# Set attention with inducing points and a hardswish layer: earlier second load, constants on another engine, the verdict's steps moved in a written-out order

## The chip, the cores and the metric

The kernel runs on one core of one Trainium2 chip. The metric is the device time of one execution in microseconds (us); lower is better. The times are the median of several executions; beside them stands one execution that the hardware profiler recorded, with its own time and its span, which runs from the first to the last instruction.

## What is computed

```python
B, N, m, C = 4, 12480, 32, 128            # x: (B, N, C), inducing: (m, C), w_in: (128, 2048), w_out: (2048, 128)

def mab(q, kv):
    s = (1 / sqrt(C)) * (q @ kv.transpose(0, 2, 1))
    a = exp(s - s.max(-1, keepdims=True))
    a /= a.sum(-1, keepdims=True) + 1e-09
    return a @ kv

h = mab(I, x)                             # I: the inducing points, once per batch
y = mab(x, h).reshape(B * N, C)           # 49920 rows of 128
u = y @ w_in
out = (u * clip(u + 3.0, 0.0, 6.0) / 6.0) @ w_out     # float32, (49920, 128)
```

## The kernel before

**Two paths.** The kernel holds a fast path, which is one straight run of instructions, and behind it a slow path, `direct_path` (from L884). The fast path does not form the hidden layer. It expands the output of the second attention and the hardswish layer in the attention weights of the 32 inducing points: a linear part, and a quadratic part that is a sum over pairs of inducing points. That holds only while some conditions are met (bounded values, sums of weights that come out as they should). The fast path counts how often they are met, and one number, the tile `bad_i`, says whether all were. At the end every engine loads `bad_i` into a register (L877) and compares it with zero (L880). If it is 0 the program ends; if it is 1, `direct_path` computes the whole result once more, straight from the definition, and writes all of `out` again.

**The order.** Tile's own scheduling is off. The string `ORDER` (L23 to L162) lists some 1590 tokens; the loop at L873 takes them one after the other and calls the function `op_<code>` with the token's numbers. That text is the program's order: each engine gets its instructions in the order of the tokens, and the waits between the engines are put in by it, so that whoever reads a buffer waits for the token that wrote it last *before it in the text*, and whoever writes a buffer waits for earlier readers. Letters at a token's end name the engine (V is VectorE, A is ScalarE, P is GpSimd). The last number or numbers of many tokens name a bank of the PSUM tile `ps` (128 partitions, 8 banks of 512 float32).

**The work.** Each of the 4 batches is cut into 6 full groups of 2048 rows and a last small one of 192 (96 partitions by 2). Per group: `X` loads x (GpSimd's queue, L408), `K` casts it to bfloat16, `T` and `Y` transpose it over TensorE, `S`, `E`, `A` and `H` are scores, exponentials and weighted sums of the first attention. Per batch, the `c` tokens make the coefficients. `cW` (L622 to L627) adds two terms into the tile `CqT` and then halves one block of it, because a pair 16 places apart is listed twice. Per group again: `Z` to `Ra` are the second attention, `W` spreads a tile by DMA (SyncE's queue, L680), `B` forms sums over pairs of inducing points in PSUM (L731, four banks at a time: `B.3.5.1.4.6` writes banks 4, 5, 6 and 7), `F` and `U` turn them into products, `l` and `q` multiply these with the coefficients (L776, L797), `v` copies the result out of PSUM (L811) and `O` writes it (SyncE's queue, L824). The result of a small group goes through one buffer, `osl`.

**The start.** `X.0.0.8.16` and `X.0.0.0.8` load the two halves of the first group. Between them in the order stands `i6`, which makes constants on GpSimd (L357 to L363). `i1` makes the identity matrix on GpSimd, `i7` and `i9` further constants there (L367 to L382). TensorE meanwhile runs `w` tokens, wide matmuls whose results are not used (L353, 28 of them ahead of the first transposes).

**The verdict.** `y1` to `y3` count conditions on VectorE into columns of `cnt`. The one on the sums takes two tokens: `yb` (L834) is a matmul that adds the row sums `s_all` of all 28 groups over blocks of 32 partitions, into columns 0 to 27 of a PSUM bank. `y0` (L839 to L841) subtracts from that bank what is due, `s_due` (16384 for a full group, 3072 for a small one), squares the difference, and counts where it is at most 4. `y4` (L865) adds the counts over the partitions, `y5` (L868, L870) compares the total with the number that all conditions together give, and writes `bad_i`. The order before ends in `yb.6 y0.6 y1.- y4.6 O.3.6.0.- y5.6`.

**The slow path.** For each of the 4 batches `direct_path` runs two loops on the chip, of 130 turns each (L940 and L971), over 96 rows of x a turn. Each turn is one chain, since every buffer there exists once: a first-loop turn loads 96 rows by DMA, transposes, multiplies with the inducing points, takes a maximum, two exponentials, transposes, multiplies and adds to the running sum. A second-loop turn does the same for the second attention and then the layer itself in float32:

```python
   993	                for jb in range(FB):                      # 16
   994	                    nc.tensor.matmul(up[:, jb, :TN], lhsT=w_in[:, jb * P : (jb + 1) * P], rhs=h[:, :])
   996	                nc.vector.tensor_scalar(g[:, :, :], up[:, :, :TN], 3.0, 0.0, op0=ALU.add, op1=ALU.max)
   997	                nc.vector.tensor_scalar(g[:, :, :], g[:, :, :], 6.0, 1.0 / 6.0, op0=ALU.min, op1=ALU.mult)
   998	                nc.vector.tensor_mul(g[:, :, :], g[:, :, :], up[:, :, :TN])
  1000	                for jb in range(FB):
  1001	                    nc.tensor.matmul(op[:TN, :C], lhsT=g[:, jb, :], rhs=w_out[:, jb, :], ...)
  1005	                nc.vector.tensor_copy(ot[:, :], op[:TN, :C])
  1006	                nc.sync.dma_start(out[bass.ds(r0 + row, TN), :], ot[:, :])
```

At a turn's end all engines wait for each other and for all transfers before they branch back.

Of the kernel before, what the change touches and what calls it, by code (L numbers as in the profile page):

```python
# [147 lines left out]
q.3.1.0.1.3 Zs.3.3 y2.- Rz.3.4.1 q.3.1.1.1.2 F.3.2.1.0.4 O.3.0.0.- B.3.2.0.0.4 v.3.1.0.3.V W.3.2 q.3.1.3.0.3 U.3.1.1  # L148
F.3.2.1.1.6 v.3.1.1.2.V Z.3.5.6 l.3.1.1.7.3 O.3.1.0.- q.3.1.3.1.3 F.3.2.0.1.4 F.3.2.0.0.0 q.3.2.1.0.2 q.3.1.2.0.7
q.3.1.2.1.7 Ze.3.5.6 O.3.0.1.- Zu.3.3 Zd.3.3 Ra.3.3 v.3.1.3.3.V B.3.3.0.4.0 l.3.2.0.3.2 U.3.2.0 Zs.3.4 W.3.3 q.3.2.0.0.3  # L150
v.3.1.2.7.A q.3.2.0.1.3 F.3.3.0.1.0 q.3.2.1.1.2 R.3.5.7 q.3.2.2.0.0 q.3.2.3.0.1 O.3.1.1.- U.3.2.1 Zu.3.4 v.3.2.0.3.A
F.3.3.0.0.4 Rl.3.5.7 v.3.2.1.2.V q.3.2.2.1.0 B.3.3.1.4.2 Zd.3.4 l.3.2.1.0.1 Rh.3.4.V q.3.3.0.0.7 Rz.3.5.6 q.3.3.1.0.6
U.3.3.0 v.3.2.2.0.V q.3.2.3.1.1 W.3.4 F.3.3.1.0.4 F.3.3.1.1.2 v.3.2.3.1.A l.3.3.0.7.6 B.3.4.0.2.4 U.3.3.1 Z.3.6.0
q.3.3.1.1.6 F.3.4.0.0.2 q.3.3.0.1.7 v.3.3.1.6.V Ze.3.6.0 Ra.3.4 q.3.3.2.0.1 q.3.3.2.1.1 F.3.4.0.1.4 O.3.2.1.- R.3.6.6
Zs.3.5 O.3.2.0.- q.3.4.0.0.2 q.3.3.3.0.3 q.3.3.3.1.3 Zu.3.5 Rl.3.6.6 Rz.3.6.0 v.3.3.0.7.A O.3.3.0.- B.3.4.1.6.4 U.3.4.0
l.3.3.1.1.3 Rh.3.5.V l.3.4.0.2.0 Zd.3.5 v.3.3.2.1.V F.3.4.1.1.4 W.3.5 F.3.4.1.0.6 v.3.3.3.3.V q.3.4.1.0.0 q.3.4.1.1.0
# [37 lines left out]
def kernel(  # L194
# [32 lines left out]
    with ExitStack() as es:
        es.enter_context(tc.manual_schedule())
# [393 lines left out]
        def op_cW(b, k):  # L622
            split = lambda t: t.rearrange("p (f i m) -> p f i m", f=4, m=M)
            nc.vector.tensor_add(  # L624
                CqT[:, :, :, :].rearrange("p f m i -> p f i m"), split(ps[:, k, :]), split(r6[:, :])
            )
            nc.vector.tensor_scalar_mul(CqT[:, 3, :, 3], CqT[:, 3, :, 3], 0.5)  # L627
# [239 lines left out]
        def op_y5(k):  # L867
            nc.vector.tensor_reduce(cs[:, :], ps[:1, k, :5], axis=AX.X, op=ALU.add)  # L868
# [1 line left out]
            nc.vector.tensor_scalar(bad_i[:, :], cs[:, :], good, None, op0=ALU.not_equal)  # L870
# [166 lines left out]
```

## Time and profile before

| what | value |
|---|---|
| median of 3 runs | 268.82 us (268.12 to 272.86) |
| the profiled execution, its own time | 269.06 us |
| its span, first to last instruction | 267.2 us |
| busy share of TensorE, VectorE, ScalarE, GpSimd | 94%, 87%, 88%, 29% |
| mean granted TensorE clock | 0.991 |
| last instruction that counts as work (`bad_i`, L870) | starts at 263.84 us |
| loads of `bad_i` into registers (L877) | five, one per engine, from 264.0 us, about 0.5 us each |

A line of the profile has the start in us, the length in us, the engine, the line of the program, the operation, and the tiles it writes and reads. PE is TensorE's matmuls, PEld its weight loads, DVE VectorE, ACT ScalarE, POOL GpSimd, SP SyncE; a "q" behind an engine is its queue or sequencer. In the list of groups the last numbers are the busy time in us and the mean of one in ns. `direct_path` is not in this trace: `bad_i` was 0.

### The profile page before, as it was taken

To read this page: it belongs to the slowest core of one execution; us is meant where nothing else is said; L and a number is where in the kernel's file an instruction comes from. 1 tells how busy PE (TensorE), PEld (TensorE's weight loads), DVE (VectorE), ACT (ScalarE), POOL (GpSimd) and SP (SyncE) were. 2 spreads that over 40 slices of the span, in tenths; PEclk is the share of its full clock that TensorE was granted. 3 is DMA by queue.
4 is the path that set the end of the run, shared out by engine and by line. 5 is a ranking of instruction groups with operands and counts; after the bars stand their busy time and mean duration, and the time that the engine had idled before them with its cause. 6 is when DMAs were issued, how large, how long until landed. Compare 5 with 4: busy or idle time off the path is not lost.

```text
span 267.2 us, 9566 instructions
## 1 busy us (share of the span) xinstructions
PE 251.7 (94%) x3941; PEld 198.7 (74%) x3941; DVE 233.2 (87%) x497; ACT 235.7 (88%) x390; POOL 78.5 (29%) x112
## 2 busy tenths in 40 slices
PE   8998979999998999999999999989998999999991
...
GB/s 129 397 345 401 411 379 49 306 287 199 230 383 348 275 55 308 208 237 398 346 308 238 266 387 27 244 54 235 44 241 285 205 127 241 150 248 255 323 226 184
DMA packets 26768, 66.68 MB, mean 250 GB/s; under 512 B 4032, under 2 KB 17120, under 8 KB 23520
## 3 DMA queue, kind: packets, MB, share of 16 engines
...
HBM read 27.67 MB, written 25.56 MB: 199 GB/s over the span
## 4 chain that ended last, share of the span: by engine, by line
PE 60%; DMA 11%; DVE 11%; ACT 9%; issue 5%; SPq 2%; POOL 2%; DVEq 0%; ACTq 0%; POOLq 0%
PE ps L797 26%; PE ps L776 6%; PE ps L731 5%; PE ps L445 5%; PE ps L418 4%; DMA d<-dk 4%; PE ps L596 4%; DMA xr<-in_x_dram 3%; PE ps L649 2%; DMA out_dram<-os 2%; PE ps L429 2%; PE ps L688 2%; ACT xb L412 2%; ACT xT L424 1%; DVE CqT L624 1%
## 5 line engine op out<-in xcount | busy, mean ns | idle before, releaser
L741 ACT ACTIVATE TF<-ps 128x1024 bf16<-128x1024 f32 (+1 forms) x100 | 97.4, 1018 | 2.6 <-PE ps L731 2.0
L750 DVE TENSOR_TENSOR TD<-TF,d 128x2048 bf16<-128x2048 bf16 (+1 forms) x52 | 60.4, 1172 | 3.8 <-DMA d<-dk 3.1
L797 PE MATMUL ps<-Cq,TD 128*128 128x128 bf16 (+1 forms) x784 | 56.7, 219 | 1.6 <-DVE TD L750 1.5
L797 PE MATMUL ps<-Cq,TF 128*128 128x128 bf16 (+1 forms) x784 | 56.9, 219 | 0.0
L797 PEld LDWEIGHTS <-TF 128*128 128x128 bf16 (+1 forms) x784 | 45.8, 98 | 6.5 <-issue 2.3
L797 PEld LDWEIGHTS <-TD 128*128 128x128 bf16 (+1 forms) x784 | 46.3, 98 | 5.2 <-DVE TD L750 3.1
L412 POOL CAST xb<-xr 128x1024 bf16<-128x1024 f32 x29 | 33.0, 1152 | 35.9 <-DMA xr<-in_x_dram 19.0
L811 ACT COPY os<-ps 128x512 f32<-128x512 f32 x65 | 37.5, 605 | 4.8 <-PE ps L797 1.5
L445 PE MATMUL ps<-xr,a 128*32 128x128 f32 x384 | 31.3, 227 | 0.1
L418 PE MATMUL ps<-ident_b,xb 128*128 128x128 bf16 x384 | 29.4, 223 | 0.6 <-ACT xb L412 0.6
L418 PEld LDWEIGHTS <-xb 128*128 128x128 bf16 x384 | 23.4, 99 | 5.2 <-issue 1.5
L445 PEld LDWEIGHTS ps<-xr,a 128*32 128x32 f32 x384 | 24.8, 109 | 2.7 <-issue 0.6
L424 DVE COPY xT<-ps 128x1024 bf16<-128x1024 bf16 x28 | 19.0, 681 | 8.2 <-PE ps L418 7.5
L412 ACT CAST xb<-xr 128x1024 bf16<-128x1024 f32 x18 | 18.9, 1056 | 7.1 <-DMA xr<-in_x_dram 7.1
L776 PE MATMUL ps<-BD,a 64*128 64x256 f32 (+1 forms) x196 | 22.9, 320 | 1.3 <-ACT os L811 1.3
L465 POOL TENSOR_TENSOR dacc<-dacc,a 128x512 f32<-128x512 f32 x11 | 15.8, 1433 | 27.4 <-ACT a L437 16.8
L811 DVE COPY os<-ps 128x512 f32<-128x512 f32 x31 | 20.9, 683 | 2.8 <-PE ps L797 2.1
L408 POOL DMA_DIRECT2D xr<-in_x_dram x25 | 13.7, 550 | 27.0 <-PE ps L445 21.6
L424 ACT COPY xT<-ps 128x1024 bf16<-128x1024 bf16 x20 | 20.3, 1027 | 1.5 <-PE ps L418 1.5
L776 PEld LDWEIGHTS ps<-BD,a 64*128 64x128 f32 (+1 forms) x196 | 14.4, 184 | 9.1 <-issue 4.6
L731 PE MATMUL ps<-z,pair 32*128 32x256 f16 (+1 forms) x400 | 21.1, 270 | 0.0
L596 PE MATMUL ps<-pr,w_ob 128*128 128x512 bf16 x64 | 20.5, 381 | 0.0
...
## 6 DMA issues: line engine op xcount, KB each, us to landing
...
xl<-in_x_dram POOLq DMA_DIRECT2D x4, 96.0 KB, 4.8
out_dram<-osl SPq DMA_DIRECT2D x4, 96.0 KB, 4.4
```

Of the source, the lines that this page charges most:

```text
L412: copier(e)(at(xb, xbl, b, g)[:p, lo:hi, :], at(xr, xl, b, g)[:p, lo:hi, :].bitcast(FP32))
L418: nc.tensor.transpose(pt[:, (i - lo) * p : (i - lo + 1) * p], at(xb, xbl, b, g)[:p, i, :], ident_b[:p, :p])
L424: copier(e)(xT_of(b, g)[:, lo * p : hi * p], ps[:, k, :].bitcast(BF16)[:, : (hi - lo) * p])
L445: nc.tensor.matmul(ps[:M, k, :C], lhsT=at(a1, a1l, b, g)[:p, i * M : (i + 1) * M], rhs=at(xr, xl, b, g)[:p, i, :], start=(i == 0), stop=(i ...
L465: veng(e).tensor_add(dacc[:, :], dacc[:, :], a)
L596: nc.tensor.matmul(ps[:, k, :], lhsT=w_ob[:, jc, :], rhs=pr_[(4 * b + jc // 4) % NPR][:, jc % 4, :, :].rearrange("p f n -> p (f n)"), star ...
L731: nc.tensor.matmul(ps[:, pairs[j // 2] + j % 2, f * w : (f + 1) * w], lhsT=pair[rows, f].rearrange("p m i -> p (m i)"), rhs=fat(z_, b, g)[ ...
L741: nc.scalar.activation(hat(TF_, b, g, h)[:, 2 * q : 2 * q + 2, :w], ps[:, k : k + 2, :w], ACT.Exp, scale=-1.0)
L750: nc.vector.tensor_mul(split(hat(TD_, b, g, h)), split(hat(TF_, b, g, h)), d.unsqueeze(2).to_broadcast([P, J, 2, w]),)
L776: nc.tensor.matmul(ps[:p, k, s2 * 2 * C : (s2 + 1) * 2 * C], lhsT=fat(a_, b, g)[rows, s * p : (s + 1) * p], rhs=BD_[b % 2][rows, 2 * i : 2 ...
L797: nc.tensor.matmul(ps[:p, k, c0 : c0 + C], lhsT=t[:, 2 * i + j, f * w + s2 * p : f * w + (s2 + 1) * p], rhs=Cq_[b % 2][:, (1 + f) if u els ...
L811: copier(e)(to[:, :, 2 * i * C : (2 * i + 2) * C], ps[:p, k, : 2 * Sh * C].rearrange("p (s w) -> p s w", s=Sh),)
```

## The change

It changes the order at the start and at the end, and the code in three places.

**Start.** `X.0.0.0.8` now stands directly behind `X.0.0.8.16`, and `i1` ahead of `X.0.2.0.16`. `i6`, `i7` and `i9` change from GpSimd to VectorE and stand later. The cast of the first small group, `K.0.6.0.2`, goes from GpSimd to ScalarE.

**End.** `O.2.6.0`, the output of the third batch's small group, goes from the last rows to just ahead of `O.3.0.0`. `y0`, `y1`, `yb`, `y4` and `y5` move up between the steps of the last full group, and use bank 7 in place of 6. A new token, `yl`, issues the register load of `bad_i` ahead of the last copy and the last output; the comparison stays at the end.

**Code.** The halving of `CqT` moves out of `cW` into a function of its own, `op_cX`. No token of the new order is named `cX`, so these four instructions (one per batch) are gone. `op_c9` can run on ScalarE, which no token asks for.

```diff
-i2.- X.0.0.8.16 i0.- w.2.4 it.- i6.P w.2.3 X.0.0.0.8 w.2.7 w.2.1 K.0.0.8.16.A X.0.1.0.16 w.2.4 K.0.0.0.8.A w.2.3 w.2.5
-X.0.2.0.16 w.2.6 w.2.4 i1.- w.2.7 w.2.5 K.0.1.0.8.A w.2.7 i3.V w.2.6 w.2.5 T.0.0.8.16.4 w.2.5 i4.2 X.0.3.0.16
+i2.- X.0.0.8.16 X.0.0.0.8 i0.- w.2.4 it.- w.2.3 w.2.7 w.2.1 K.0.0.8.16.A X.0.1.0.16 i1.- X.0.2.0.16 w.2.4 K.0.0.0.8.A
+w.2.3 w.2.5 w.2.6 w.2.4 w.2.7 w.2.5 K.0.1.0.8.A w.2.7 i6.V i3.V w.2.6 w.2.5 T.0.0.8.16.4 w.2.5 i4.2 X.0.3.0.16
...
-q.3.5.2.0.6 U.3.5.1 Ra.3.6 v.3.5.1.2.A B.3.6.0.4 O.3.4.1.- l.3.5.1.6.3 F.3.6.0.0.4 q.3.5.3.0.3 q.3.5.2.1.6 O.2.6.0.-
-O.3.5.0.- U.3.6.0 q.3.5.3.1.3 q.3.6.0.0.0 v.3.5.2.6.V q.3.6.0.1.0 v.3.5.3.3.A O.3.5.1.- l.3.6.0.0 v.3.6.0.0.V yb.6 y0.6
-y1.- y4.6 O.3.6.0.- y5.6
+v.3.5.0.0.A q.3.5.2.0.6 U.3.5.1 y0.7 y1.- Ra.3.6 v.3.5.1.2.A yb.7 B.3.6.0.4 O.3.4.1.- l.3.5.1.6.3 F.3.6.0.0.4
+q.3.5.3.0.3 q.3.5.2.1.6 O.3.5.0.- U.3.6.0 y4.7 q.3.5.3.1.3 q.3.6.0.0.0 v.3.5.2.6.V y5.7 q.3.6.0.1.0 v.3.5.3.3.A
+O.3.5.1.- l.3.6.0.0 yl v.3.6.0.0.V O.3.6.0.-
...
+
+        def op_cX(b):
             nc.vector.tensor_scalar_mul(CqT[:, 3, :, 3], CqT[:, 3, :, 3], 0.5)
...
+        def op_yl():
+            bad.append(
+                nc.values_load(
+                    bad_i[0:1, 0:1], min_val=0, max_val=1, skip_runtime_bounds_check_because="a comparison gives 0 or 1"
+                )
+            )
...
-    with tc.If(bad > 0, preferred_fallthrough_block=False):
+    with tc.If(bad[0] > 0, preferred_fallthrough_block=False):
```

The lines of the changed kernel are some 1 to 10 higher than those of the kernel before (L839 is now L845, L834 is L840, L880 is L890).

VectorE's last rows before, from the last full group's last product on: `cnt` and `r` are the counts and a scratch tile, and what an instruction waits for stands in brackets.

```order
L750 TENSOR_TENSOR TD_106<-TF_105,d_101 128x2048 [waits Activation_49]
L750 TENSOR_TENSOR TD_107<-TF_103,d_102 128x2x192 [waits DMAHW7_49,DMAHW6_49,Activation_49]
L811 COPY os<-ps 128x2x256 [waits DMAHW4_49,PE_49]
L811 COPY osl_109<-ps 96x256 [waits DMAHW1_49,PE_49]
L839 TENSOR_TENSOR r_134<-ps,s_due 128x28 [waits PE_49]
L840 TENSOR_TENSOR r_134<-r_134 128x28 [waits DVE_49]
L841 TENSOR_SCALAR r_134,cnt<-r_134 128x28 [waits DVE_49]
L846 TENSOR_SCALAR r_134,cnt<-z_all 128x28 [waits DVE_49]
L868 TENSOR_REDUCE cs<-ps 1x1 [waits PE_49]
L870 TENSOR_SCALAR bad_i<-cs 1x1 [waits DVE_49]
L877 TENSOR_LOAD bad_i [waits DVE_49]
```

And now:

```order
L756 TENSOR_TENSOR TD_106<-TF_105,d_101 128x2048 [waits Activation_49]
L845 TENSOR_TENSOR r_134<-ps,s_due 128x28 [waits DVE_49]
L846 TENSOR_TENSOR r_134<-r_134 128x28 [waits DVE_49]
L847 TENSOR_SCALAR r_134,cnt<-r_134 128x28 [waits DVE_49]
L852 TENSOR_SCALAR r_134,cnt<-z_all 128x28 [waits DVE_49]
L756 TENSOR_TENSOR TD_107<-TF_103,d_102 128x2x192 [waits DMAHW7_49,DMAHW0_49,Activation_49]
L817 COPY os<-ps 128x2x256 [waits DMAHW5_49,PE_49]
L874 TENSOR_REDUCE cs<-ps 1x1 [waits PE_49]
L876 TENSOR_SCALAR bad_i<-cs 1x1 [waits DVE_49]
L880 TENSOR_LOAD bad_i [waits DVE_49]
L817 COPY osl_109<-ps 96x256 [waits PE_49]
```

The subtraction of `y0` (L839, now L845) stood behind a wait for TensorE, which is the one for `yb`; now it waits only for VectorE itself.

TensorE at the place where `yb` now stands, between the last `q` matmuls of a full group and the pair sums of the small one:

```order
L803 LDWEIGHTS TF_105
L803 MATMUL ps<-Cq_120,TF_105 128x128
L840 MATMUL ps<-s_all,blk 128x28 [waits DVE_49,Activation_49]
L737 LDWEIGHTS pair
L737 MATMUL ps<-z_98,pair 128x96
```

Before, the same matmul was the second-last of the fast path on TensorE:

```order
L776 MATMUL ps<-BD_122,a_93 96x256
L834 MATMUL ps<-s_all,blk 128x28 [waits DVE_49]
L865 MATMUL ps<-cnt,ones 1x5 [waits DVE_49]
L877 TENSOR_LOAD bad_i [waits DVE_49]
```

It now has the rest of the full group's matmuls and all of the small group's behind it, and waits for VectorE and for ScalarE, which makes the last row sums.

GpSimd at the start, from its first load on, before:

```order
L408 DMA xr_68<-in_x_dram 128x1024
L357 MEMSET ones 128x128
L358 MEMSET r_134 128x128
L359 MEMSET mask 128x512
...
L363 MEMSET mask 32x128
L408 DMA xr_68<-in_x_dram 128x1024
L408 DMA xr_69<-in_x_dram 128x2048
L408 DMA xr_70<-in_x_dram 128x2048
masks.py:197 MEMSET ident 128x128
```

And now:

```order
L409 DMA xr_68<-in_x_dram 128x1024 x2
L409 DMA xr_69<-in_x_dram 128x2048
masks.py:197 MEMSET ident 128x128
masks.py:199 ISA
masks.py:199 AFFINE_SELECT ident<-ident 128x128
L409 DMA xr_70<-in_x_dram 128x2048
```

Eleven memsets have left the place between the two halves, and the third group's load stands behind the identity matrix.

More of the change, by code (lines that the diff above doesn't have):

```diff
@@ L23 @@
 ORDER = """
-i2.- X.0.0.8.16 i0.- w.2.4 it.- i6.P w.2.3 X.0.0.0.8 w.2.7 w.2.1 K.0.0.8.16.A X.0.1.0.16 w.2.4 K.0.0.0.8.A w.2.3 w.2.5
-X.0.2.0.16 w.2.6 w.2.4 i1.- w.2.7 w.2.5 K.0.1.0.8.A w.2.7 i3.V w.2.6 w.2.5 T.0.0.8.16.4 w.2.5 i4.2 X.0.3.0.16
-Y.0.0.8.16.4.V w.2.5 K.0.1.8.16.A i5.2.V i8.- X.0.4.0.16 T.0.0.0.8.1 w.2.4 T.0.1.0.8.0 T.0.1.8.16.3 i7.P Y.0.1.0.8.0.V
-i9.P Y.0.0.0.8.1.A K.0.2.0.8.P Y.0.1.8.16.3.A S.0.0.0.8.6 S.0.1.0.8.4 S.0.0.8.16.6 E.0.0.0.16.6 T.0.2.0.8.2 A.0.0.0.8.7
+i2.- X.0.0.8.16 X.0.0.0.8 i0.- w.2.4 it.- w.2.3 w.2.7 w.2.1 K.0.0.8.16.A X.0.1.0.16 i1.- X.0.2.0.16 w.2.4 K.0.0.0.8.A
+w.2.3 w.2.5 w.2.6 w.2.4 w.2.7 w.2.5 K.0.1.0.8.A w.2.7 i6.V i3.V w.2.6 w.2.5 T.0.0.8.16.4 w.2.5 i4.2 X.0.3.0.16
+Y.0.0.8.16.4.V w.2.5 K.0.1.8.16.A i5.2.V i8.- i9.V X.0.4.0.16 T.0.0.0.8.1 w.2.4 T.0.1.0.8.0 T.0.1.8.16.3 Y.0.1.0.8.0.V
+Y.0.0.0.8.1.A K.0.2.0.8.P Y.0.1.8.16.3.A S.0.0.0.8.6 S.0.1.0.8.4 S.0.0.8.16.6 E.0.0.0.16.6 T.0.2.0.8.2 A.0.0.0.8.7
 K.0.2.8.16.P Y.0.2.0.8.2.V S.0.1.8.16.4 T.0.2.8.16.5 K.0.3.0.8.V X.0.6.0.2 E.0.1.0.16.4 K.0.3.8.16.A Y.0.2.8.16.5.A wi.-
-D.0.0.V A.0.0.8.16.7 S.0.2.0.8.1 T.0.3.0.8.6 D.0.1.V X.0.5.0.16 K.0.4.0.8.A A.0.1.0.8.0 K.0.6.0.2.P T.0.3.8.16.2
-Y.0.3.0.8.6.V A.0.1.8.16.0 S.0.2.8.16.1 S.0.3.0.8.3 K.0.4.8.16.P E.0.2.0.16.1 Y.0.3.8.16.2.V S.0.3.8.16.3 T.0.6.0.2.6
+i7.V D.0.0.V A.0.0.8.16.7 S.0.2.0.8.1 T.0.3.0.8.6 D.0.1.V X.0.5.0.16 K.0.4.0.8.A A.0.1.0.8.0 T.0.3.8.16.2 Y.0.3.0.8.6.V
+A.0.1.8.16.0 S.0.2.8.16.1 S.0.3.0.8.3 K.0.4.8.16.P E.0.2.0.16.1 Y.0.3.8.16.2.V S.0.3.8.16.3 K.0.6.0.2.A T.0.6.0.2.6
 H.0.0.7 w.2.7 D.0.2.V E.0.3.0.16.3 T.0.4.0.8.2 A.0.2.0.8.7 w.2.1 Y.0.6.0.2.6.A D.0.3.V wh.0.V H.0.1.0 Y.0.4.0.8.2.A
@@ L147 @@
 v.3.0.2.6.V Ze.3.4.1 Ra.3.2 q.3.1.0.0.3 Rh.3.3.V q.3.0.3.1.7 v.3.0.3.7.A R.3.4.0 l.3.1.0.3.2 Rl.3.4.0 B.3.2.1.4.6
[L148 to L156, printed above, removed]
@@ L157 @@
-U.3.4.1 q.3.4.0.1.2 B.3.5.0.4.6 q.3.4.3.0.3 q.3.4.2.0.1 q.3.4.3.1.3 v.3.4.1.0.A F.3.5.0.0.4 q.3.5.0.0.0 Zs.3.6
-F.3.5.0.1.6 q.3.4.2.1.1 O.3.3.1.- B.3.5.1.4.6 Zu.3.6 Zd.3.6 l.3.4.1.1.3 v.3.4.0.2.V Ra.3.5 Rh.3.6.V O.3.4.0.- W.3.6
-l.3.5.0.0.2 q.3.5.1.0.2 U.3.5.0 v.3.4.3.3.V y3.- v.3.4.2.1.V F.3.5.1.1.6 q.3.5.1.1.2 q.3.5.0.1.0 F.3.5.1.0.4 v.3.5.0.0.A
-q.3.5.2.0.6 U.3.5.1 Ra.3.6 v.3.5.1.2.A B.3.6.0.4 O.3.4.1.- l.3.5.1.6.3 F.3.6.0.0.4 q.3.5.3.0.3 q.3.5.2.1.6 O.2.6.0.-
-O.3.5.0.- U.3.6.0 q.3.5.3.1.3 q.3.6.0.0.0 v.3.5.2.6.V q.3.6.0.1.0 v.3.5.3.3.A O.3.5.1.- l.3.6.0.0 v.3.6.0.0.V yb.6 y0.6
@@ L162 @@
-y1.- y4.6 O.3.6.0.- y5.6
+q.3.1.0.1.3 Zs.3.3 y2.- Rz.3.4.1 q.3.1.1.1.2 F.3.2.1.0.4 O.2.6.0.- O.3.0.0.- B.3.2.0.0.4 v.3.1.0.3.V W.3.2 q.3.1.3.0.3
+U.3.1.1 F.3.2.1.1.6 v.3.1.1.2.V Z.3.5.6 l.3.1.1.7.3 O.3.1.0.- q.3.1.3.1.3 F.3.2.0.1.4 F.3.2.0.0.0 q.3.2.1.0.2
+q.3.1.2.0.7 q.3.1.2.1.7 Ze.3.5.6 O.3.0.1.- Zu.3.3 Zd.3.3 Ra.3.3 v.3.1.3.3.V B.3.3.0.4.0 l.3.2.0.3.2 U.3.2.0 Zs.3.4 W.3.3
+q.3.2.0.0.3 v.3.1.2.7.A q.3.2.0.1.3 F.3.3.0.1.0 q.3.2.1.1.2 R.3.5.7 q.3.2.2.0.0 q.3.2.3.0.1 O.3.1.1.- U.3.2.1 Zu.3.4
+v.3.2.0.3.A F.3.3.0.0.4 Rl.3.5.7 v.3.2.1.2.V q.3.2.2.1.0 B.3.3.1.4.2 Zd.3.4 l.3.2.1.0.1 Rh.3.4.V q.3.3.0.0.7 Rz.3.5.6
@@ new lines @@
+q.3.3.1.0.6 U.3.3.0 v.3.2.2.0.V q.3.2.3.1.1 W.3.4 F.3.3.1.0.4 F.3.3.1.1.2 v.3.2.3.1.A l.3.3.0.7.6 B.3.4.0.2.4 U.3.3.1
+Z.3.6.0 q.3.3.1.1.6 F.3.4.0.0.2 q.3.3.0.1.7 v.3.3.1.6.V Ze.3.6.0 Ra.3.4 q.3.3.2.0.1 q.3.3.2.1.1 F.3.4.0.1.4 O.3.2.1.-
+R.3.6.6 Zs.3.5 O.3.2.0.- q.3.4.0.0.2 q.3.3.3.0.3 q.3.3.3.1.3 Zu.3.5 Rl.3.6.6 Rz.3.6.0 v.3.3.0.7.A O.3.3.0.- B.3.4.1.6.4
+U.3.4.0 l.3.3.1.1.3 Rh.3.5.V l.3.4.0.2.0 Zd.3.5 v.3.3.2.1.V F.3.4.1.1.4 W.3.5 F.3.4.1.0.6 v.3.3.3.3.V q.3.4.1.0.0
+q.3.4.1.1.0 U.3.4.1 q.3.4.0.1.2 B.3.5.0.4.6 q.3.4.3.0.3 q.3.4.2.0.1 q.3.4.3.1.3 v.3.4.1.0.A F.3.5.0.0.4 q.3.5.0.0.0
@@ new lines @@
+Zs.3.6 F.3.5.0.1.6 q.3.4.2.1.1 O.3.3.1.- B.3.5.1.4.6 Zu.3.6 Zd.3.6 l.3.4.1.1.3 v.3.4.0.2.V Ra.3.5 Rh.3.6.V O.3.4.0.-
+W.3.6 l.3.5.0.0.2 q.3.5.1.0.2 U.3.5.0 v.3.4.3.3.V y3.- v.3.4.2.1.V F.3.5.1.1.6 q.3.5.1.1.2 q.3.5.0.1.0 F.3.5.1.0.4
+v.3.5.0.0.A q.3.5.2.0.6 U.3.5.1 y0.7 y1.- Ra.3.6 v.3.5.1.2.A yb.7 B.3.6.0.4 O.3.4.1.- l.3.5.1.6.3 F.3.6.0.0.4
+q.3.5.3.0.3 q.3.5.2.1.6 O.3.5.0.- U.3.6.0 y4.7 q.3.5.3.1.3 q.3.6.0.0.0 v.3.5.2.6.V y5.7 q.3.6.0.1.0 v.3.5.3.3.A
+O.3.5.1.- l.3.6.0.0 yl v.3.6.0.0.V O.3.6.0.-
@@ L225 @@
     bad_i = keep.tile([1, 1], I32, name="bad_i")
+    bad = []
     with ExitStack() as es:
@@ L502, in op_c9 @@
         def op_c9(b, e):
-            veng(e).tensor_scalar_mul(HTs_[b % 2][:, :], HT[:, :], scale)
+            if e == "A":
+                nc.scalar.mul(HTs_[b % 2][:, :], HT[:, :], scale)
+            else:
+                veng(e).tensor_scalar_mul(HTs_[b % 2][:, :], HT[:, :], scale)
         def g_of(k):
@@ L875 @@
             ops[code](*[int(a) if a.isdigit() else a for a in args])
-    bad = nc.values_load(
-        bad_i[0:1, 0:1], min_val=0, max_val=1, skip_runtime_bounds_check_because="a comparison gives 0 or 1"
-    )
-    with tc.If(bad > 0, preferred_fallthrough_block=False):
+    with tc.If(bad[0] > 0, preferred_fallthrough_block=False):
         direct_path(tc, x, inducing, moe_w_in, moe_w_out, out, scale)
```

## Prediction

> **What bounds the kernel now.** First the page's list of engines and the chain of waits at the end; from these two alone the change would look like a matter of 1%.
>
> ```profile
> span 267.2 us, 9566 instructions
> PE 251.7 (94%) x3941; PEld 198.7 (74%) x3941; DVE 233.2 (87%) x497; ACT 235.7 (88%) x390; POOL 78.5 (29%) x112
> ```
>
> TensorE is busy 94% of the span, so at most the two ends leave room. The chain that ended last, from 258 us on:
>
> ```profile
> 258.31 3.78 DMA out_dram<-osl
> ...
> 262.19 0.42 DVE osl L811
> ...
> 263.18 0.20 DVE r L846 x2
> 263.38 0.04 issue
> 263.43 0.21 PE ps L865 x2
> 263.63 0.02 issue
> 263.66 0.16 DVE cs L868
> 263.82 0.02 issue
> 263.84 0.14 DVE bad_i L870
> ```
>
> The last copy waits for a small output that was issued late, then the verdict runs in nine short steps, and the verdict ends the chain. The profiled execution took 269.06 us: 1.86 lie outside its span, and it is 0.24 above the median.
>
> The start, from the timeline (start, length):
>
> ```profile
> 1.24 0.76 POOL L408 DMA_DIRECT2D xr<-in_x_dram  x1 [0.79 <-POOLq L1021]
> 3.92 1.59 POOL L408 DMA_DIRECT2D xr<-in_x_dram  x3
> 9.67 0.65 PEld L418 LDWEIGHTS <-xb 128*128 128x128 bf16 x8
> 11.23 1.99 ACT L412 CAST xb<-xr 128x1024 bf16<-128x1024 f32 x2 [1.44 <-DMA xr<-in_x_dram]
> 12.32 0.46 PEld L418 LDWEIGHTS <-xb 128*128 128x128 bf16 x8 [0.30 <-ACT xb L412]
> ```
>
> **What decides: the order of the verdict.** In the new text `y0` stands ahead of `yb`. `y0` reads bank 7 of PSUM, and the instruction that wrote it last before that in the text is not `yb` but the pair sum `B.3.5.1.4.6`, which writes banks 4 to 7. VectorE takes its instructions in order and `y0` has no wait for TensorE left; `yb` is the one that waits, for `y0` to have read. So the sums `yb` makes come too late for the only reader, in every execution and by construction, not by a race.
>
> What `y0` then finds are sums of two logarithms of attention weights, which `y1` itself demands to be at most 32 each. They differ from the due 16384 or 3072 by thousands, where 2 is allowed. Not one of the 128 by 28 entries counts; the total misses by 3584; `bad_i` becomes 1. Then every engine loads 1 and enters `direct_path`, which the trace of before never shows. Its result overwrites the fast path's, including whatever the missing halving (`cX`) would do to it. So the time is the fast path plus four times 130 turns of two loops.
>
> **The fast path's own edits** are priced quickly, as they vanish beside that. Start: 11 memsets leave GpSimd between the first two rows above, so the second half is issued about 1.9 us sooner, and the third load with it; ScalarE's casts at 11.23 can start that much sooner, but TensorE reaches its transposes behind the `w` matmuls only at 9.67, and waits at 12.32 are 0.30: gain between 0 and 1.9, I take 0.7. The memsets on VectorE lie in its idle 5 us before the identity's cast. The four halvings gone:
>
> ```profile
> L627 DVE TENSOR_SCALAR CqT<-CqT 128x32 bf16<-128x32 bf16 x4 | 1.9, 487 | 0.1
> DVE osl L811 <- DMA out_dram<-osl: 1.8, 1, 1.8
> 260.53 0.36 PE L776 MATMUL ps<-BD,a 64*96 64x256 f32 x1
> DMA to landing us min/median/max: 2.2/3.0/3.8
> ```
>
> Between 0 and 1.9, VectorE being rarely last; 0.5. End: with the earlier small output, the last copy starts when TensorE ends at 260.89 and not at 262.19: 1.3. Sum 2.5, so the fast path's end would be reached near 264.7 of the span.
>
> **The slow path, from the nearest rows.** No row shows it, so every term has two ends.
>
> *Transfers.* A turn loads 48 KB, and the second loop writes 48 KB. The last small output (96 KB, an idle queue) landed after the shortest time above, 2.2. Nearest rows: 1.8 and 4.4.
>
> ```profile
> os<-in_inducing_dram SPq DMA_DIRECT2D x1, 16.0 KB, 1.8
> out_dram<-osl SPq DMA_DIRECT2D x4, 96.0 KB, 4.4
> ```
>
> I take 2.2 each, since nothing else is in flight.
>
> *Turning back.* The nearest thing is the program's own end: the last output (262.63 plus 2.2) lands at 264.8, and until 267.2 all engines only meet. That is 2.4. Low end 0.7, the waits of SyncE's sequencer for TensorE's there; high end 4.8, two such meetings.
>
> ```profile
> 262.63 0.34 SPq L824 DMA_DIRECT2D out_dram<-osl  x1
> SPq L1032 <- PEq L1032: 0.7, 2, 0.5
> ```
>
> *A float32 matmul* runs as two passes: the one token `yb` shows x2.
>
> ```profile
> 260.81 0.30 PEld L834 LDWEIGHTS ps<-s_all,blk 128*128 128x128 f32 x2
> 260.81 0.40 PE L834 MATMUL ps<-s_all,blk 128*128 128x28 f32 x2
> L688 PE MATMUL ps<-e,blk 128*128 128x512 f32 x24 | 12.6, 527 | 0.0
> L445 PE MATMUL ps<-xr,a 128*32 128x128 f32 x384 | 31.3, 227 | 0.1
> 10.86 0.24 PE L346 MATMUL ps<-ident,os 32*128 32x32 f32 x1
> ```
>
> 0.40 for 28 columns; 384 columns more cost 0.30 a pass, so 68 more cost 0.11 in both: 0.51 alone. Back to back it is at least the two weight loads, 0.30. I take 0.40, 6.4 for a burst of 16. A transpose is 0.25.
>
> *TensorE's clock.* Row first:
>
> ```profile
> 0.00:6.60 6.60, 5.40 (x13) 1.94 (x14) 0.50 (x2) 2.33 (x2) 5.34 (x22) 1.00 0.44 127
> 36.00:40.00 4.00, 4.00 (x79) 3.11 (x75) 3.66 (x8) 3.48 (x5) 1.97 (x4) 0.66 1.06 424
> 264.00:267.20 3.20, 0.00 (x0) 0.00 (x0) 0.00 (x0) 0.00 (x0) 0.00 (x0) 0.81 0.07 19
> L353 PE MATMUL ps<-TD 128*128 128x512 bf16 x48 | 14.9, 448 | 1.2 <-DVE TD L340 1.2
> ```
>
> The first 13 wide matmuls after idleness take 5.40, 0.42 each, in a kernel where the same 512 columns later take half; and the granted clock is 0.66 and 0.81 after stretches without matmuls. A slow-path turn is mostly idle for TensorE. So each burst starts slow: in 5.4 us it does what takes 2.7 at speed, then the other 3.7: 9.1 a burst (6.4 all fast, 12.8 all slow), and the scattered matmuls cost double. The Trainium skill's "TensorE: Matmul & The Clock Gate" (Part 1, The HAM clock gate) says the clock falls to half after an idle window of about 3.4 us and comes back after as long of sustained work; by its 3.4 a burst would be 8.1 (an estimate from that page), 1040 us less over all turns. The trace agrees in kind, not in the length.
>
> *Small steps* on VectorE and ScalarE are 0.14 to 0.28:
>
> ```profile
> 262.53 0.17 DVE L839 TENSOR_TENSOR r<-ps,s_due 128x28 f32<-128x28 f32 x1
> L437 ACT ACTIVATE a1l<-ps 96x64 fp32r<-96x64 f32 x4 | 0.9, 233 | 0.0
> L557 DVE TENSOR_SCALAR r<-ps 128x512 f32<-128x512 f32 x4 | 2.7, 686 | 0.2 <-PE ps L548 0.2
> L463 DVE COPY dacc<-a 128x512 f32<-128x512 f32 x1 | 0.4, 428 | 0.0
> ```
>
> I take 0.2, and 0.03 a hand-over (the "issue" pieces of the chain). The three wide operations over 1536 columns: from 28 to 512 columns the rows rise by 0.51 out of PSUM and 0.26 within SBUF, so 1.8, 1.0 and 1.8: 4.5.
>
> *Second-loop turn:* transfers 4.4; two transposes and two matmuls 1.5, slow 3.0; ten small VectorE steps 2.0; one exponential 0.23; 15 hand-overs 0.4; bursts 18.2; wide 4.5; turning back 2.4. Sum 35.1. *First-loop turn:* 2.2 + 3.0 + six steps 1.2 + two exponentials 0.46 + 0.3 + 2.4 = 9.6. Together 44.7, times 520 = 23,240. Reloading both weights, entering the loops and the fast path add some 300. **23,500 us.**
>
> Ends: all low, 1.8 a transfer, 0.7 back, bursts at 0.30 a matmul, 22.5 + 6.0 a pair of turns: 15,100. All high, 4.4, 4.8 and slow bursts at 1.02 a matmul, 56 + 14: 37,000.
>
> **Rivals.** *The verdict comes out true* (the other side). Place: `y0`. Price: none of the slow path; the end is 264.7 of span, 266.6 with what lies outside, 266 beside the median. It decides if anything puts `yb`'s sums into bank 7 before `y0` reads. For it: before, the same check gives 0 with bank 6. Against it: `yb` waits for `y0`. 0.04.
>
> *The slow path at full clock*: bursts 6.4, scattered matmuls 1.5, 28.2 + 8.1 = 36.3 a pair, 19,200 us. For it: the granted clock reads 1.00 in the very window with the slow matmuls, so it may be the first use that is slow, not idleness. Against: 0.66 and 0.81 after idle stretches. 0.25. It is the case in which the Trainium skill's rule on the clock gate fails here.
>
> *Turning back costs far more*, 10 us a turn: then 1040 times 7.6 more, 31,400. For it: nothing in the trace branches back, so no row bounds it. Against: the whole end of the program fits in 2.4. 0.10. The Trainium skill's "Runtime: NRT & Kernel Launch" (Instruction fetch mechanics) says a taken branch whose target is not in the two blocks at hand stalls for a fetch; no run here shows it.
>
> **How the numbers follow.** Forecast 0.61 at 23,500, full clock 0.25, costly return 0.10, verdict true 0.04. The range takes the middle of what the ends allow and both slow rivals: 16,000 to 33,000. About 2% is what a measurement of this kernel can tell from no change; the true verdict lies within it (266 against 268.82), with a little of its weight beyond: faster 0.01, same 0.03, slower 0.96.
>
> **What would show it.** Right: L845 of `y0` runs ahead of L840's matmul; the registers load 1; lines of `direct_path` fill the trace, with 520 turns each of L950 and L981; TensorE's busy share falls from 94% to under 60%. The steps: 16 matmuls of L1004 in about 9 us, L1006 to L1008 in 4.5, loads landing in 2.2, 2.4 between a turn's last landing and the next load. Wrong: a span near 265 with no line past L890; or a turn whose time is not set by the chain of one buffer each.

## The result and the profile after

The changed kernel takes 18,294.76 us (median of 4 runs, 18,288.88 to 18,298.4) where the kernel before takes 268.48 beside it (268.12 to 272.86): 68.17 times as long, with an interval of 68.04 to 68.30. The profiled execution took 18,295.47 us, of which 1.87 lie outside the span. Here and below, ratios leave out executions that took over 1.5% more than the fastest of their kernel, while medians and ranges keep them.

The head of the page after, with the row of TensorE's granted clock over 40 slices:

```profile
span 18293.6 us, 163033 instructions
PE 9082.1 (50%) x43447; PEld 7808.7 (43%) x43466; DVE 4601.7 (25%) x11979; ACT 652.5 (4%) x1951; POOL 78.0 (0%) x96
PEclk7556666666555666666655566666665556666666
```

TensorE's share falls from 94% to 50%, ScalarE's from 88% to 4%, and the clock is granted at 0.5 to 0.6 nearly throughout (0.604 in the mean). In the clock row one sees four batches: a short stretch of fives (the first loop), then a long one of sixes (the second).

The end of the fast path, from the timeline after (start, length, and in brackets what the engine waited for):

```profile
256.55 0.18 DVE L845 TENSOR_TENSOR r<-ps,s_due 128x28 f32<-128x28 f32 x1
...
256.88 0.38 PE L840 MATMUL ps<-s_all,blk 128*128 128x28 f32 x2 [1.54 <-DVE r L845]
...
260.46 0.14 DVE L876 TENSOR_SCALAR bad_i<-cs 1x1 int32<-1x1 f32 x1
...
262.40 0.34 SPq L830 DMA_DIRECT2D out_dram<-osl  x1
265.21 0.36 SPq L912 DMA_DIRECT2D d_w_in<-in_moe_w_in_dram  x1
```

The subtraction of `y0` (L845) starts at 256.55 and the matmul of `yb` (L840), which should have made its input, at 256.88. TensorE has even waited 1.54 us for that subtraction. In this execution its clock also fell to half at 257.90 and came back at 261.31 (0.72 in the mean from 256 to 262 us, where the repaired kernel's last 7 us of work have 1.00); that is one execution of each, and whether the misplaced pair brings the fall about is not shown. The last output is issued at 262.40, 0.23 earlier than before, and then, where the program used to end, the first instruction of `direct_path` (L912) loads its weights.

Four rows from the list of groups, which carry the new time, and the two kinds of transfers of a turn:

```profile
L1006 DVE TENSOR_SCALAR d_g<-d_u 128x1536 f32<-128x1536 f32 x520 | 913.9, 1758 | 3627.6 <-PE d_u L1004 3627.6
L1015 DVE COPY d_ot<-d_o 96x128 f32<-96x128 f32 x520 | 149.2, 287 | 3300.8 <-PE d_o L1011 3300.8
L1008 DVE TENSOR_TENSOR d_g<-d_g,d_u 128x1536 f32<-128x1536 f32 x520 | 912.5, 1755 | 18.1
...
L1007 DVE TENSOR_SCALAR d_g<-d_g 128x1536 f32<-128x1536 f32 x520 | 498.9, 959 | 18.0
...
d_x<-in_x_dram SPq DMA_DIRECT2D x1040, 48.0 KB, 1.7
out_dram<-d_ot SPq DMA_DIRECT2D x520, 48.0 KB, 1.5
```

The counts say that both loops ran in full: 1040 loads, 520 outputs. The idle time in the first two rows is VectorE's wait for the two bursts of 16 float32 matmuls: 3627.6 / 520 = 6.98 us and 3300.8 / 520 = 6.35 us a burst.

The first batch's two loops as stretches (length, busy time of PE, PEld, DVE, ACT and POOL, granted clock, DMA share, GB/s):

```profile
274.00:1228.00 954.00, 239.29 (x781) 90.45 (x781) 236.48 (x1174) 67.22 (x260) 0.00 (x0) 0.50 0.02 7
1230.00:4773.00 3543.00, 1967.71 (x9090) 1811.04 (x9091) 855.79 (x1690) 36.82 (x130) 0.00 (x0) 0.62 0.01 4
```

Divided by 130 turns, a first-loop turn takes 7.34 us. The stretch of the second loop is cut a little short at its ends, so its turn is better read from the copies of the result, one per turn (count; shortest, median and longest in ns; start of the first and the last in us):

```profile
L1015 DVE COPY d_ot<-d_o x130: 286/287/289, 1252.5 to 4774.8; 96x128 f32<-96x128 f32 x130
```

From the first to the last are 129 turns, so one takes 27.30 us. The pair takes 34.6, and 520 pairs are some 18,010 of the 18,294 us.

One second-loop turn:

```profile
1252.81 0.36 SPq L1016 DMA_DIRECT2D out_dram<-d_ot  x1
1255.47 0.33 SPq L924 DMA_DIRECT2D d_x<-in_x_dram  x1
...
1257.31 0.40 PE L926 MATMUL d_tr<-d_ident,d_x 96*128 96x96 f32 x1 [4.85 <-DMA d_x<-in_x_dram]
...
1262.00 6.77 PE L1004 MATMUL d_u<-d_hT,d_w_in 128*128 128x96 f32 x32 [0.35 <-DVE d_hT L1001]
1268.81 1.76 DVE L1006 TENSOR_SCALAR d_g<-d_u 128x1536 f32<-128x1536 f32 x1 [6.87 <-PE d_u L1004]
...
1273.41 6.20 PE L1011 MATMUL d_o<-d_w_out,d_g 128*96 128x128 f32 x32 [4.63 <-DVE d_g L1008]
1279.64 0.29 DVE L1015 COPY d_ot<-d_o 96x128 f32<-96x128 f32 x1 [6.29 <-PE d_o L1011]
```

It reads as one chain: output issued, 2.66 us until the next load, 1.84 until TensorE starts on what it brought, 4.7 of small steps, a burst of 6.77, wide steps, a burst of 6.20. No two of them overlap.

The granted clock in that turn, in stretches (it is the number behind the five busy times):

```profile
1255.00:1262.00 7.00, 2.00 (x6) 1.18 (x7) 1.83 (x9) 0.28 (x1) 0.00 (x0) 0.50 0.02 7
1262.00:1268.00 6.00, 6.00 (x28) 6.00 (x29) 0.00 (x0) 0.00 (x0) 0.00 (x0) 0.50 0.00 0
1268.00:1269.00 1.00, 0.77 (x6) 0.61 (x5) 0.19 (x1) 0.00 (x0) 0.00 (x0) 0.88 0.00 0
1269.00:1271.00 2.00, 0.00 (x0) 0.00 (x0) 1.97 (x2) 0.00 (x0) 0.00 (x0) 1.00 0.00 0
1271.00:1272.00 1.00, 0.00 (x0) 0.00 (x0) 0.96 (x2) 0.00 (x0) 0.00 (x0) 0.83 0.00 0
1272.00:1278.00 6.00, 4.59 (x22) 4.59 (x23) 1.35 (x1) 0.00 (x0) 0.00 (x0) 0.50 0.00 0
1278.00:1279.00 1.00, 1.00 (x8) 1.00 (x8) 0.00 (x0) 0.00 (x0) 0.00 (x0) 0.76 0.00 0
```

The first burst starts at 1262.00 with the clock at half. A mean of 0.88 in the slice from 1268 to 1269 means that full clock came 0.24 into it (0.24 by 0.5 and 0.76 by 1.0), 6.2 us after the burst's start, when 0.5 us of it were left. VectorE then has 4.5 us of wide steps; full clock stands through the first two of them, and by the 0.83 it is lost again at 1271.66, 2.9 us after the last matmul. So the second burst starts at half as well and is at full clock only from 1278.48, 5.1 us after its start. Full clock comes just as the work for it ends, twice a turn.

The three changes of the clock lie 3.42 us (1268.24 to 1271.66) and 6.82 us (1271.66 to 1278.48) apart: one step of 3.41 us and two. The next ones in this trace, at 1281.90, 1295.55 and 1298.97, lie on the same steps.

### The profile page after: what moved, and what is told of

Its sections match the earlier page's. It is cut to its first block, busy times and chain, and to the rows that moved or that the text cites. A ratio compares the mean times of both kernels' runs of the same rounds, so it can differ in the third digit from the quotient of the medians.

```text
span 18293.6 us, 163033 instructions
## 1 busy us (share of the span) xinstructions
PE 9082.1 (50%) x43447; PEld 7808.7 (43%) x43466; DVE 4601.7 (25%) x11979; ACT 652.5 (4%) x1951; POOL 78.0 (0%) x96
## 5 line engine op out<-in xcount | busy, mean ns | idle before, releaser
L1011 PE MATMUL d_o<-d_w_out,d_g 128*96 128x128 f32 x16640 | 3252.8, 385 | 2409.3 <-DVE d_g L1008 2409.3
L1011 PEld LDWEIGHTS d_o<-d_w_out,d_g 128*96 128x96 f32 x16640 | 3140.8, 254 | 2494.6 <-DVE d_g L1008 2494.6
L1004 PE MATMUL d_u<-d_hT,d_w_in 128*128 128x96 f32 x16640 | 3579.5, 414 | 182.1 <-DVE d_hT L1001 182.1
L1004 PEld LDWEIGHTS d_u<-d_hT,d_w_in 128*128 128x128 f32 x16640 | 3494.3, 325 | 307.6 <-DVE d_hT L1001 307.6
L926 PE MATMUL d_tr<-d_ident,d_x 96*128 96x96 f32 x1040 | 409.5, 394 | 4286.8 <-DMA d_x<-in_x_dram 4284.8
L1006 DVE TENSOR_SCALAR d_g<-d_u 128x1536 f32<-128x1536 f32 x520 | 913.9, 1758 | 3627.6 <-PE d_u L1004 3627.6
L1015 DVE COPY d_ot<-d_o 96x128 f32<-96x128 f32 x520 | 149.2, 287 | 3300.8 <-PE d_o L1011 3300.8
L1008 DVE TENSOR_TENSOR d_g<-d_g,d_u 128x1536 f32<-128x1536 f32 x520 | 912.5, 1755 | 18.1
L1007 DVE TENSOR_SCALAR d_g<-d_g 128x1536 f32<-128x1536 f32 x520 | 498.9, 959 | 18.0
L999 PE MATMUL d_h<-d_aT,d_Ha 32*128 32x96 f32 x1040 | 383.7, 470 | 175.6 <-DVE d_aT L997 175.6
L971 PE MATMUL d_h<-d_x,d_aT 96*32 96x128 f32 x1040 | 329.3, 420 | 145.1 <-DVE d_aT L969 145.1
```

The source lines that it names most:

```text
L926: nc.tensor.transpose(tr[:, :TN], xt[:, :], ident[:TN, :TN])
L971: nc.tensor.matmul(hp[:M, :C], lhsT=aT[:, :], rhs=xt[:, :])
L999: nc.tensor.matmul(hp[:, :TN], lhsT=Ha[:, :], rhs=aT[:, :])
```

## The experiments

Seven kernels. Four of them, those with a ratio, ran on one chip beside 35 runs of the kernel before (268.09 in the median). The kernel before with its two tokens swapped and the last two kernels are single executions on another chip, beside one of 266.47.

### The verdict's two tokens in their right order

```diff
-v.3.5.0.0.A q.3.5.2.0.6 U.3.5.1 y0.7 y1.- Ra.3.6 v.3.5.1.2.A yb.7 B.3.6.0.4 ...
+v.3.5.0.0.A q.3.5.2.0.6 U.3.5.1 Ra.3.6 v.3.5.1.2.A yb.7 y0.7 y1.- B.3.6.0.4 ...
```

> The changed kernel with one edit: the tokens y0.7 y1.- go behind yb.7; the constants on VectorE, the early register load and the missing halving stay. (Its fast path leaves out the halving of the pairs listed twice, as the changed kernel's does.) If the order of y0 and yb alone makes the verdict false: the slow path is gone and the time is near 265, that is 268.5 less the 2.4 us by which the changed kernel's last full group already ran ahead and 1.3 for the last copy, with about 0.3 for steps that no longer end the chain. If instead the constants that VectorE makes (s_due, blk, ones) spoil the count, or the early load reads bad_i before it is written: still 18,295.

Measured: 266.53 us (263.63 to 277.12, 13 runs), ratio 0.9915 [0.9871, 0.9959] to the kernel before. The whole factor of 68 is gone with `yb` set ahead of its reader; the constants on VectorE, bank 7, the early register load and the missing halving are all still there. Of the theories only the order is left.

### The two tokens swapped in the kernel before

```diff
-... O.3.5.1.- l.3.6.0.0 v.3.6.0.0.V yb.6 y0.6
+... O.3.5.1.- l.3.6.0.0 v.3.6.0.0.V y0.6 yb.6
```

> The kernel before with two tokens swapped at its end, y0.6 ahead of yb.6, and nothing else of the change. If this order alone decides: the slow path runs, 18,295 within 15 us. If it takes something else of the change besides (constants on VectorE, the early register load, the bank): 268.

Measured: 18,278.28 us, 16.5 below the changed kernel and so just outside the 15 that were expected. The timeline shows the same picture at the old place:

```profile
263.55 0.17 DVE L839 TENSOR_TENSOR r<-ps,s_due 128x28 f32<-128x28 f32 x1
...
263.77 0.41 PE L834 MATMUL ps<-s_all,blk 128*128 128x28 f32 x2 [2.40 <-DVE r L839]
```

TensorE could have run `yb` 2.40 us sooner and waits for `y0` to have read the bank. So the swap is enough by itself, and nothing else of the change is needed for it. The two experiments together, taking it away and doing it alone, settle the cause.

### The changed kernel with both repairs

The order as in the first experiment, and the halving put back:

```diff
-... cW.0.2 Z.0.4.0 ...
+... cW.0.2 cX.0 Z.0.4.0 ...        (and cX.1, cX.2, cX.3 behind the other three cW)
```

> As the run with the verdict in order, and the halving cX put back behind each cW: everything that the change meant, computed in full. If the four halvings lie mostly off the path that sets the end: 265.3, at most 0.5 above that run. If VectorE is on the path there: up to 1.9 above it, near 267. Against the kernel before: 0.985 to 0.992.

Measured: 268.22 us (265.97 to 329.66), ratio 0.9986 [0.9945, 1.0026], above the expected 0.985 to 0.992. What remains of the change, once the sums come in time, can't be told from nothing. Beside the first experiment's 0.9915 the halvings would be worth 0.7%, but the two intervals overlap, so their price stays open; their busy time, 1.9 us in all, is as much.

### The start alone

The kernel before with the changed rows of the start, its end and its `cW` untouched:

```diff
-i2.- X.0.0.8.16 i0.- w.2.4 it.- i6.P w.2.3 X.0.0.0.8 ...
+i2.- X.0.0.8.16 X.0.0.0.8 i0.- w.2.4 it.- w.2.3 ... i6.V i3.V ... i9.V ... i7.V
```

> The kernel before with the change's start alone (second half of x issued first, constants on VectorE, the small group's cast on ScalarE). If a shift at the start is carried to the end by a TensorE that is busy 94%: 1.0 to 1.6 us less than before, near 267, as the first exponential starts 1.25 us sooner in the changed kernel's trace. If transfers bound the first 40 us and even it out: 268.5, no difference.

Measured: 268.24 us (265.01 to 274.49), ratio 0.9941 [0.9896, 0.9986]. Of the kernels that do the whole computation, halvings included, this is the only one whose interval lies below 1. From its timeline:

```profile
7.37 1.05 ACT L412 CAST xb<-xr 128x1024 bf16<-128x1024 f32 x1 [0.81 <-DMA xr<-in_x_dram]
8.51 0.65 PEld L418 LDWEIGHTS <-xb 128*128 128x128 bf16 x8
...
13.63 0.60 ACT L437 ACTIVATE a<-ps 128x512 fp32r<-128x512 f32 x1
```

The last of these rows is the first exponential, and before it was:

```profile
14.99 0.60 ACT L437 ACTIVATE a<-ps 128x512 fp32r<-128x512 f32 x1
```

The second half of x is cast from 7.37 on (8.74 before), and the first exponential starts 1.36 us sooner, where the prediction took 0.7 out of a range of 0 to 1.9. The weight loads of the first transposes also start sooner, at 8.51 against 9.67, but that can't be put down to the change: they stand behind 28 `w` matmuls, of which 12 ran at half pace before and 7 here, and this number differs from trace to trace (9 in the trace of the two tokens swapped, which has the old start: weight loads at 8.99, first exponential at 14.95 all the same).

The ratio gives 1.6 us (0.4 to 2.8 by its interval). It is not borne out by the other pair of kernels that differ in the start alone: the one with both repairs (new start) and the next one (old start) both stand at 0.9986. So what the start is worth stays open.

### The end alone

The repaired kernel with the old rows of the start:

```diff
-i2.- X.0.0.8.16 X.0.0.0.8 i0.- w.2.4 it.- w.2.3 ... i6.V i3.V ... i9.V ... i7.V
+i2.- X.0.0.8.16 i0.- w.2.4 it.- i6.P w.2.3 X.0.0.0.8 ...
```

> The kernel before with the change's end alone: verdict moved up and in the right order, early register load, the small output a batch sooner; the start as before and the halving kept. If the last copy's wait and the nine verdict steps set the end: 1.3 to 2.0 us less, near 266.8. If the last output's landing sets it in both: 1.3 at most, 267.2. If the verdict's matmuls cost as much inside the group as they save: 268.5.

Measured: 267.79 us (266.69 to 273.67), ratio 0.9986 [0.9955, 1.0017]: no gain that can be told from nothing. Its trace shows where the gain goes. The end of its timeline, then a row of the waits of SyncE's queue from 255 us on, then the last small output in that stretch (KB, us from issue to landing):

```profile
258.92 0.14 DVE L876 TENSOR_SCALAR bad_i<-cs 1x1 int32<-1x1 f32 x1
...
260.45 0.34 SPq L830 DMA_DIRECT2D out_dram<-osl  x1
```

```profile
SPq L1042 <- DMA out_dram<-osl: 1.8, 1, 1.8
```

```profile
out_dram<-osl SPq DMA_DIRECT2D x1, 96.0 KB, 4.0
```

The verdict is ready at 258.92 and not at 263.84, and the last output is issued at 260.45 and not at 262.63. But that output now lands after 4.0 us, where it took 2.2 before (the last full output ahead of it has landed by 262.6, so why it takes so long is only in part explained); so it lands at 264.5 instead of 264.8, and the program's end waits 1.8 us for it. Before, the end came 3.2 us behind the verdict; now it comes 1.1 behind this landing. So the last output is issued 2.2 us sooner and takes 1.8 longer, and the verdict, 4.9 us earlier, no longer sets the end. By the ratio 0.4 us are left (-0.5 to 1.2). The two traces are one execution each, with spans 1.6 us apart, so they show where the time goes, not how much of it.

### TensorE kept busy between the two bursts

The next two kernels take the slow path of the changed kernel apart. Here 16 wide matmuls on a tile of zeros, whose result is never read, fill VectorE's wide steps:

```diff
+        busy = kp.tile([P, 512], BF16, name="d_busy")
+        nc.vector.memset(busy[:, :], 0.0)
...
                     nc.tensor.matmul(up[:, jb, :TN], lhsT=w_in[:, jb * P : (jb + 1) * P], rhs=h[:, :])
+                tr = ps.tile([P, 512], FP32, name="d_tr")
+                for _ in range(16):
+                    nc.tensor.matmul(tr[:, :], lhsT=busy[:, :P], rhs=busy[:, :])
```

> The changed kernel with 16 wide matmuls of no use in each turn of the slow path's second loop, between the two bursts of 16, while VectorE does its three wide steps (4.5 us). If idleness is what slows the second burst, through the granted clock of 0.50: it starts at full clock, shrinks from 6.2 to about 3.4 us, as the last passes of a burst at clock 1.0 take 0.10 against 0.20, and the time falls by 520 times 2.8 to about 16,840; the first burst stays near 6.8. If a float32 pass takes 0.2 at any clock: 18,295, or more by what the added matmuls delay.

Measured: 16,515.76 us, 1,779 less, with 16 matmuls more in every turn. A turn, its granted clock in the second burst (the third number from the end), the rows of the groups for its two bursts, and the copies of the result in the first batch:

```profile
2000.99 0.63 PE L1009 MATMUL d_tr<-d_busy 128*128 128x512 bf16 x1 [0.33 <-issue]
...
2001.41 5.62 PE L1006 MATMUL d_u<-d_hT,d_w_in 128*128 128x96 f32 x32
...
2006.87 3.19 PE L1009 MATMUL d_tr<-d_busy 128*128 128x512 bf16 x14
...
2011.66 3.73 PE L1016 MATMUL d_o<-d_w_out,d_g 128*96 128x128 f32 x32 [1.61 <-DVE d_g L1013]
```

```profile
2011.00:2015.00 4.00, 3.33 (x30) 3.34 (x31) 0.61 (x1) 0.00 (x0) 0.00 (x0) 1.00 0.00 0
```

```profile
L1016 PE MATMUL d_o<-d_w_out,d_g 128*96 128x128 f32 x16640 | 1941.8, 275 | 838.5 <-DVE d_g L1013 838.5
...
L1011 DVE TENSOR_SCALAR d_g<-d_u 128x1536 f32<-128x1536 f32 x520 | 914.0, 1758 | 3183.8 <-PE d_u L1006 3183.8
```

```profile
L1020 DVE COPY d_ot<-d_o x130: 287/287/289, 1251.0 to 4333.1; 96x128 f32<-96x128 f32 x130
```

The same 16 matmuls of the second burst now take 3.73 us a turn (1941.8 / 520), not 6.20. That is the price at full clock: 0.23 a matmul, against 0.42 in a burst that is at half but for its last 0.5 us (6.77 / 16). The first burst also fell, from 6.98 to 6.12 (3183.8 / 520), which had not been expected: full clock now comes 4.0 us after its start (2005.41 against 2001.41) and not 6.2. Two of the 16 extra matmuls were placed ahead of this burst; whether that is why was not tested. Those 0.86 times 520 are 447 us, and they account for the 324 by which the run beat its expectation, and more.

By the copies a turn now takes 23.89 us and took 27.30 before. These are seven and eight of the clock's steps of 3.41 us, and 520 times the 3.41 between them is some 1,770 of the 1,779. All four batches of both traces show these turns, and so does the kernel before with its tokens swapped (27.30). So in these loops the turn settles on a whole number of steps, as the price of a burst depends on where among the steps it starts. How a turn comes to settle was not tested.

### Two pieces a turn

```diff
-            with tc.For_i(0, N, TN) as row:
-                xt, xT = load(r0 + row)
...
+            with tc.For_i(0, N, 2 * TN) as row2:
+                for row in (row2, row2 + TN):
+                    xt, xT = load(r0 + row)
...
```

in both loops, so half as many turns back.

> The changed kernel with two pieces of 96 rows in each turn of both loops of the slow path, so half as many turns (65 in place of 130), the same work. If turning back costs the 1.15 us from a landing to the next load's issue that the trace shows: 520 of 1040 returns go, 600 us; in the second loop the skipped return also hides the output's 1.5 and the load's 1.8, 260 times 3.3, 860 more: about 16,830. If it costs the 2.4 of the prediction: 260 by 2.4 more twice, about 16,200. If the return is hidden behind the landing anyway: only the 860, 17,430.

Measured: 14,721.74 us, below all three figures. It saves 3,573, some 2,100 more than the 1,460 of the first of them. Two bursts of the first kind in neighbouring pieces:

```profile
3011.21 0.29 DVE L1017 COPY d_ot<-d_o 96x128 f32<-96x128 f32 x1 [5.32 <-PE d_o L1013]
...
3012.51 3.81 PE L1006 MATMUL d_u<-d_hT,d_w_in 128*128 128x96 f32 x32 [0.35 <-DVE d_hT L1003]
...
3037.07 7.07 PE L1006 MATMUL d_u<-d_hT,d_w_in 128*128 128x96 f32 x32
```

A second piece's first burst starts 1.01 us after the first piece's copy ends (3011.50); in the changed kernel it is 9.2, from 1252.79 to 1262.00. Its load, its transpose and its scores have run beside the first piece's work. And as the burst before has ended only 1.3 us earlier (the copy at 3011.21 stands right behind it), this one runs at full clock (granted 1.00 from 3010 to 3020): 3.81 against 7.07 in a first piece. So halving the turns did three things, and only one of them was the return. By loops the saving can be read off the copies: a second-loop turn of two pieces takes 42.66 us where two turns took 54.61, and 260 times that difference is some 3,100; the first loop has the other 470 or so. How either splits among the three was not measured apart.

## Why the prediction was right or wrong, point by point

**Sign and cause: right.** `y0` ahead of `yb` sends every execution down the slow path. The first two experiments show it from both sides, and the trace shows L845 ahead of L840, the first lines of `direct_path`, and 520 turns of each loop. The step that decided was reading what had written bank 7 last *in the text*. Which numbers `y0` then found there stands in no trace; only the order and the verdict do.

**Size: 18,295 against 23,500, within the range.** The forecast had 44.7 us for a pair of turns, where 34.6 were measured. The 10.1 between them, by terms:

| term | predicted | measured | times | difference |
|---|---|---|---|---|
| two bursts of 16 float32 matmuls | 18.2 | 13.3 (6.98 + 6.35) | 520 | 2,530 us |
| turning back | 2.4 | 1.2 | 1040 | 1,250 |
| transfers, both loops | 6.6 | 4.9 (1.7 + 1.7 + 1.5) | 520 | 880 |
| three wide VectorE steps | 4.5 | 4.47 | 520 | 0 |
| small steps and hand-overs, both loops | 10.6 | 9.5 (what is left of 34.6) | 520 | 570 |

They add up to 5,230 us, by which the forecast's 23,240 for 520 pairs lies above the measured 18,010; they must, as the last row is what is left.

**The bursts: the step that failed was the price of one matmul.** The prediction read 0.40 us off the one token `yb`, took that for full clock, and set 0.30, "at least the two weight loads", as the low end. Both were read off one matmul that runs alone. Back to back the passes overlap (275 ns each with TensorE kept busy, and 32 of them in 3.73 us): 0.23 a matmul at full clock, 0.42 nearly all at half. So the low end itself was too high. The second half of the step was nearly right: each burst starts slow, for 5.4 us by the prediction, and for 6.2 and 5.1 by the clock. With these 5.4 and the true price a burst would have been 6.4 (5.4 at half do 2.7 of the 3.73), near the 6.98 and 6.35 of the table; with the price of 0.40 the forecast came out 4.9 high a turn. That 5.4 came so near is partly luck: it is the slow stretch at the start of one execution, and in the other traces that stretch has 7 to 14 slow matmuls where it had 12.

**The rival "full clock at 19,200" lies closer to the time than the forecast does, and it is false.** Its bursts of 6.4 were the wrong price at the wrong clock; the granted clock is 0.50 through 11.3 (6.2 and 5.1) of the 13 us of bursts in a turn. At full clock the two would take some 3.75 each, 5.8 a turn less, and the whole some 15,300 (an estimate from the 3.73 above). A near number had no bearing on its mechanism.

**The clock: right in kind, by a partly wrong row.** A gap of 4.5 us between the bursts costs the clock, as it is lost 2.9 us after the last matmul. But a stretch without matmuls is not needed for it: the prediction's row of 0.66 (36 to 40 us) stands behind a pause of only 1.4 us (34.0 to 35.4), and the fall at 257.90 in the changed kernel behind one of 1.54. In the three steps of 3.41 us ahead of the falls TensorE was busy for 2.0, 1.9 and, in the slow path, 0.5 us.

The Trainium skill's "TensorE: Matmul & The Clock Gate" (Part 1, The HAM clock gate) lets the clock fall after an idle window of about 3.4 us and return after as long of sustained work. By it a burst of 16 at the price of 0.40 would have been 8.1, and at the measured price 5.4 (an estimate from that page: 3.4 us at half do 1.7 of the 3.73), where 6.77 and 6.20 were measured. The trace agrees in kind; it differs in that full clock took 6.2 and 5.1 us to come, and in the two falls that had no idle window. The page also says that the window runs freely and is not tied to the work, so that the way back depends on where in it the work starts. The trace agrees: the changes lie on steps of 3.41 us, and full clock came at the end of the first step that the burst filled from end to end (1264.83 to 1268.24, 1275.07 to 1278.48).

**Turning back: right in kind, half the size.** The output of the turn above is issued at 1252.81, lands after 1.5, and the next load is issued at 1255.47: 1.16. In the first loop it is 1.2 from the last step to the next load. From the waits of SyncE's queue in the first batch's second loop (total, times, longest):

```profile
SPq L981 <- DMA out_dram<-d_ot: 88.6, 129, 0.7
SPq L981 <- PEq L981: 62.8, 258, 0.4
```

Two meetings with TensorE's sequencer a turn, together 62.8 / 129 = 0.49 us: about the 0.7 of the program's end, which the prediction had as its low end, and not the 2.4. The 2.4 was the wrong row: in the kernel before no wait for the last landing (264.8) is on record, as the register loads (from 264.0) and the comparison still had to come, so that what it priced was the tail of the verdict. In "The end alone", where SyncE does wait for the landing, the end comes 1.1 us behind it. The rival of 10 us a turn falls.

**Transfers: mis-sized.** 1.7 and 1.5, below the low end of 1.8 and below the 2.2 that was taken. The 2.2 was read off a transfer of 96 KB, twice as large, and its queue was not idle, as the prediction has it: a full output issued at 260.80 was still under way (the DMA engines are busy for 83% of the stretch from 262 to 264 us).

**Wide and small steps: right.** 1.76, 0.96 and 1.76 against 1.8, 1.0 and 1.8.

**The fast path's own edits: 2.5 us predicted, of which little can be shown.** With the sums in time the first experiment gives 266.53, near the 266 of the rival "the verdict comes out true"; that rival is false all the same, as nothing put the sums there in time. Piece by piece: start 1.6 by one comparison (predicted 0.7) and nothing by the other, end 0.4 with an interval from -0.5 to 1.2 (predicted 1.3), halvings open (predicted 0.5). The step that failed for the end: the prediction let the last copy start earlier and took the whole shift as gain, where the output behind it, issued 2.2 us sooner, took 4.0 us and not 2.2.
